# Layer 1's third and fourth chunk: the first product by seven block products, with sums of weights made on DVE and ACT

## The chip, the cores and the metric

One NeuronCore of a Trainium2 chip runs the kernel. Its engines work from queues of their own: PE (TensorE, matrix products into PSUM; PEld is its weight load), DVE (VectorE), ACT (ScalarE), POOL (GpSimd) and SP (SyncE, which issues most DMAs). Each takes its instructions strictly in the order in which the program left them, and waits for the others by semaphores. The metric is device time in microseconds (us) of one execution.

## What is computed

Attention over q, k, v (sparse masks), then a first layer (mixing along the tokens, then a two-product feed-forward), then the second layer, "layer 1" in the code. The change lies in the last part of it:

```python
def _moe2_ref(x, w_ch1, w_ch2):
    X = np.fft.fft(x, axis=1)
    X = np.fft.fft(X, axis=2)
    mixed = np.real(X).astype(np.float32)
    u = x + mixed
    mu = np.mean(u, axis=-1, keepdims=True)
    var = np.mean((u - mu) ** 2, axis=-1, keepdims=True)
    un = (u - mu) / np.sqrt(var + 1e-06)
    ch = np.maximum(un @ w_ch1, 0.0) @ w_ch2
    return (u + ch).astype(np.float32)
```

x is 4 batches of 576 tokens by 512; w_ch1 is 512 by 2048, w_ch2 2048 by 512.

## The kernel before

The 2304 tokens lie in 18 tiles of 128 tokens; `chunk_tiles` (L643) groups them in chunks: 0 to 3 are one batch each but for its last tokens (4 tiles, 512 tokens), chunk 4 holds the rest of all four batches (2 tiles, 256 tokens). `SEQ` (L847) runs the two layers' chunks one after the other: layer 0 in the order 0, 1, 2, 4, 3, layer 1 in the order 0, 1, 2, 3, 4. A pair (1, 2) below is layer 1, chunk 2, which is the layer's third.

`ffn` (L787) is one chunk's feed-forward. It works in two halves h of the 2048 hidden columns, eight blocks of 128 (`HW`) each. A half has a first product, one PSUM tile of 128 hidden columns by the chunk's tokens after the other, and a second product, which adds the half's eight blocks into one PSUM tile for each token tile. All values are kept as two fp16 parts, high and low, and a product is three matrix multiplications (high by high, high by low, low by high): L807 to L809 in the first product (12 for a tile, 96 for a half), L833 to L835 in the second (24 for a token tile, 96 for a half of a 4-tile chunk).

- A tile of the first product leaves PSUM by an eviction pair: ACT's relu into `gh` (L813), then DVE's rest into `gl` (L814). The PSUM pool `pf1` has two buffers, so PE starts tile i+2 only when tile i's pair is through.
- A token tile of the second product leaves by one DVE instruction, `ub` (L841, `ur` for chunk 4), from the pool `pf2`, also two buffers; in layer 1's second half SP then writes it out (L844).
- The operands of layer 1's first product come from `prep2` (L755): mean and variance, `un` on DVE (L777), its high part on ACT (L781), its low part on POOL (L782), and `put_T` (L595) turns both by DMA transposes that SP issues (L612) into `ut`. `ut` is single, so these transposes wait until the chunk before has ended its first products.
- `fft_gen` (L646) does batch b's two Fourier transforms on PE, ACT and DVE and adds them to `ub`; it must be through before `prep2` of that batch.
- `w_half` and `w_scale` (L202, L186) bring the weights in as two fp16 parts. They live in slots S0 to S32; S24 to S31 are free in layer 1.

The order of the instructions comes from two side lanes (`Lane`, L53), "w" for weights and "s" for the rest: `tick` (L944), called from the feed-forward's loops, steps them by rates for each chunk (`RATES`, L50; first number weights, second the rest), and a scheduler behind it fixes each engine's queue from that, with a higher priority for the evictions. A lane holds at a `guard` until a flag of the feed-forward is set, and the feed-forward pulls what it needs with `until`.

Of the kernel before, what the change touches and what calls it, by code (L numbers as in the profile page):

```python
# [7 lines left out]
F32 = mybir.dt.float32  # L8
# [61 lines left out]
def fused_kernel(ctx: ExitStack, tc: tile.TileContext, ql, kl, vl, vr, qs, ks, vs, uraw, vraw,  # L70
# [131 lines left out]
    def w_half(l, kind, src, names, h):  # L202
        m0 = h * HW
        row = 2 * kind + h
        sls = [slot(names[0])]
        for i in range(HW):
            sls.append(slot(names[i + 1]))
            w = sls[i + 1].bitcast(F32).rearrange("p a n -> p (a n)")
            to_f32(take(src, m0 + i), w)
            fetch()  # L210
            A.activation(out=sls[0][:, 0, :].bitcast(BF16), in_=w, func=AF.Square, accum_out=wst[:, row, i:i + 1])  # L211
            yield
        w_scale(l, kind, h)
        yield
        for i in range(HW):
            m = m0 + i
            w = sls[i + 1].bitcast(F32).rearrange("p a n -> p (a n)")
            sc = wsc[:, l, row, i:i + 1]
            split_hi(sls[i][:, 0, :], w, sc)
            split_lo(sls[i][:, 1, :], w, sc, sls[i][:, 0, :])  # L220
            W[l, kind, m] = sls[i]
            flags.add(f"w{l}{kind}{m}")
            yield

    ap_ctx = ExitStack()
# [369 lines left out]
    def put_T(key, j, hi, lo):  # L595
        if j == 0:
            UT[key] = [utp.tile([128, 4, 512], F16, tag=f"ut{i}", name=f"ut{i}") for i in range(2)]
# [157 lines left out]
    def prep2(c, tiles):  # L755
# [18 lines left out]
        yield  # L774
        for j, t in enumerate(tiles):
            un = fp.tile([128, 512], F32, tag="un", name="un")
            V.tensor_scalar(out=un, in0=utile(t), scalar1=mv[:, j, 0:1], scalar2=rs[:, j:j + 1],  # L777
# [3 lines left out]
            A.activation(out=hi, in_=un, func=AF.Copy)  # L781
            G.tensor_tensor(out=lo, in0=un, in1=hi, op=ALU.subtract)  # L782
            put_T((1, c), j, hi, lo)
            yield
        flags.add(f"p1{c}")

    def ffn(l, c, tick):  # L787
        tiles = chunk_tiles(c)
        n = 128 * len(tiles)
        until(f"p{l}{c}")  # L790
        uh, ul = UT[l, c]
        for h in range(2):
            gh = gp.tile([128, HW, 512], F16, tag="gh", name="gh")
            gl = gp.tile([128, HW, 512], F16, tag="gl", name="gl")
            subs = SUB if l == c == h == 0 else ((0, len(tiles)),)
            for s0, s1 in subs:
                cols = slice(128 * s0, 128 * s1)
                n = 128 * (s1 - s0)
                for i in range(HW):
# [12 lines left out]
                    with tc.high_priority(HP):  # L812
                        A.activation(out=gh[:, i, cols], in_=ps[:, 0:n], func=AF.Relu)  # L813
                        V.scalar_tensor_tensor(out=gl[:, i, cols], in0=ps[:, 0:n], scalar=0.0, in1=gh[:, i, cols],  # L814
                                               op0=ALU.max, op1=ALU.subtract)
            flags.add(f"e{l}{c}{h}1")
            until(f"w{l}1{h * HW}")
# [31 lines left out]
    def prep(q):  # L849
        l, c = SEQ[q]  # L850
        if q >= 2:
            yield from guard("e%d%d11" % SEQ[q - 2])
        yield from (prep2 if l else prep1)(c, chunk_tiles(c))

    def weights():
# [15 lines left out]
        yield from guard("e0311")  # L871
        yield from w_half(1, 1, w22, n[16:24] + n[32:], 1)

    def side():
# [15 lines left out]
        yield from prep(6)  # L890
        yield from fft_gen(3)
        for q in (7, 8, 9):
            yield from prep(q)

    def open_phase2():
        ap_ctx.close()
        fp = ctx.enter_context(tc.tile_pool(name="fft", bufs=2))
        fft["pool"] = fp
        fft["w"] = ctx.enter_context(tc.tile_pool(name="vsl", bufs=1))
        th = fp.tile([128, 2, 3, 290], F32R, tag="th", bufs=1, name="th")  # L900
# [26 lines left out]
    for l in range(2):  # L927
        for c in range(5):
            owner[f"p{l}{c}"] = sl
        for m in range(NW):  # L930
            owner[f"w{l}0{m}"] = owner[f"w{l}1{m}"] = wl
    ml = Lane(load_mix(), flags)
    first_loads()
# [194 lines left out]
```

## Time and profile before

| what | us |
|---|---|
| median of three runs | 972.61 (969.4 to 978.28) |
| the profiled execution, its own time | 973.36 |
| its span, first to last instruction | 971.4 |
| PE busy | 928.4 (96%) |
| DVE busy | 532.5 (55%) |
| ACT busy | 360.9 (37%) |
| POOL busy | 61.0 (6%) |

A busy PE is a modelled span of pipelined products, so it tells only where PE has no gaps. The shares are means over the whole span; what a change in one stage is worth is read from that stage.

### The profile page before, as it was taken

The numbers are of one execution on the slowest core, as the hardware profiler recorded it, in microseconds if no ns is written. First come the engines' busy times: TensorE is split into PE (matmuls) and PEld (weight loads), VectorE is DVE, ScalarE is ACT, GpSimd is POOL, SyncE is SP. The second block draws the span as 40 slices with busy tenths as digits, with TensorE's granted clock in tenths as the row PEclk, the third lists the DMA queues.
The fourth block names the chain that finished last, engine by engine and source line by source line (L and its number), as shares of the span: only waits on it lengthen the run. The fifth ranks groups of instructions, "written<-read, shape, count | busy, mean of one in ns | idle before, by whom it ended". The sixth has DMA issues, their size and how long they took to land.

```text
span 971.4 us, 13694 instructions
## 1 busy us (share of the span) xinstructions
PE 928.4 (96%) x5264; PEld 520.9 (54%) x5264; DVE 532.5 (55%) x1346; ACT 360.9 (37%) x885; POOL 61.0 (6%) x91
## 2 busy tenths in 40 slices
PE   5958899999999999999999989999999999999998
PEld 4746654556545665466445445555554444444465
DVE  4588788834352346862878998994245212222122
ACT  4577687724131434631446454231122101111011
POOL 0010011000000001100110400011001000100000
PEclk9969999999999999999999999999999999999999
DMA  9357666332201102601323520011002001200100
GB/s 315 121 180 250 207 213 206 103 116 95 64 7 37 39 3 95 175 21 35 97 90 127 131 65 1 1 36 53 1 1 55 33 1 11 76 1 1 52 15 22
DMA packets 60464, 76.53 MB, mean 79 GB/s; under 512 B 38064, under 2 KB 43440, under 8 KB 60400
## 3 DMA queue, kind: packets, MB, share of 16 engines
q1 hardware_dynamic: 51376, 42.53, 15.5%
q0 software_dynamic: 9024, 33.14, 10.6%
q8 instruction: 41, 0.67, 0.3%
q14 instruction: 23, 0.19, 0.1%
HBM read 60.18 MB, written 7.08 MB: 69 GB/s over the span
## 4 chain that ended last, share of the span: by engine, by line
PE 52%; DMA 3%; DVE 3%; ACT 1%; issue 1%; SPq 0%; ACTq 0%; DVEq 0%
PE f L833 8%; PE f L834 8%; PE f L835 8%; PE f L807 8%; PE f L808 8%; PE f L809 8%; DMA raw<-in_w 2%; DMA ut<-lo 1%; DVE wslot L156 1%; PE bk L689 1%; PE bk L688 1%; PE bk L690 1%; ACT wslot L153 1%; PE bk L698 0%; SPq L612 0%
## 5 line engine op out<-in xcount | busy, mean ns | idle before, releaser
L807 PE MATMUL f<-ut,wslot 128*128 128x512 f16 (+1 forms) x672 | 235.6, 351 | 8.0 <-DVE gl L814 7.6
L808 PE MATMUL f<-ut,wslot 128*128 128x512 f16 (+1 forms) x672 | 235.2, 350 | 1.1 <-DMA ut<-lo 1.1
L809 PE MATMUL f<-ut,wslot 128*128 128x512 f16 (+1 forms) x672 | 235.1, 350 | 0.0
L833 PE MATMUL f<-wslot,gh 128*128 128x512 f16 x576 | 218.1, 379 | 0.6 <-DVE ub L841 0.3
L834 PE MATMUL f<-wslot,gh 128*128 128x512 f16 x576 | 218.1, 379 | 0.1
L835 PE MATMUL f<-wslot,gl 128*128 128x512 f16 x576 | 218.1, 379 | 0.0
L813 ACT ACTIVATE gh<-f 128x512 f16<-128x512 f32 (+1 forms) x168 | 89.5, 533 | 300.9 <-PE f L809 300.3
L814 DVE SCALAR_TENSOR_TENSOR gl<-f,gh 128x512 f16<-128x512 f32 (+1 forms) x168 | 102.9, 612 | 145.5 <-ACT gh L813 144.9
L841 DVE SCALAR_TENSOR_TENSOR ub<-f,ivt,ub 128x512 f32<-128x512 f32 x64 | 47.9, 748 | 127.6 <-PE f L835 127.4
L808 PEld LDWEIGHTS <-wslot 128*128 128x128 f16 x672 | 66.1, 98 | 66.2 <-issue 12.4
L807 PEld LDWEIGHTS <-wslot 128*128 128x128 f16 x672 | 66.3, 99 | 59.3 <-issue 4.0
L809 PEld LDWEIGHTS <-wslot 128*128 128x128 f16 x672 | 66.0, 98 | 58.6 <-issue 0.9
L835 PEld LDWEIGHTS <-gl 128*128 128x128 f16 x576 | 56.4, 98 | 67.0 <-issue 0.3
L833 PEld LDWEIGHTS <-gh 128*128 128x128 f16 x576 | 57.0, 99 | 63.2 <-issue 0.2
L834 PEld LDWEIGHTS <-gh 128*128 128x128 f16 x576 | 56.7, 98 | 62.5 <-issue 1.3
L153 ACT ACTIVATE wslot<-wslot,wsc 128x512 f16<-128x512 f32 x64 | 46.0, 719 | 41.9 <-DVE wslot L156 21.2
L133 ACT ACTIVATE wslot<-raw 128x512 f32<-128x512 f32 x64 | 42.7, 675 | 29.4 <-DMA raw<-in_w 29.0
L160 POOL DMA_DIRECT2D raw<-in_w x61 | 33.3, 546 | 316.7 <-DVE wslot L137 62.1
L156 DVE SCALAR_TENSOR_TENSOR wslot<-wslot,wsc 128x512 f16<-128x512 f32 x64 | 48.7, 760 | 6.6 <-ACT wslot L153 6.4
L211 ACT ACTIVATE wslot<-wslot 128x512 bf16<-128x512 f32 x64 | 40.3, 629 | 20.9 <-DVE wslot L137 16.8
L377 ACT ACTIVATE P<-bk,mx 108x64 f32<-108x64 f32 (+2 forms) x126 | 31.3, 329 | 39.2 <-DVE mx L372 35.9
L137 DVE SCALAR_TENSOR_TENSOR wslot<-raw,wslot 128x512 int32<-128x512 int32 x64 | 44.4, 697 | 0.1
(225 smaller groups left out, 952.2 us busy)
## 6 DMA issues: line engine op xcount, KB each, us to landing
raw<-in_w POOLq DMA_DIRECT2D x61, 512.0 KB, 3.9
q<-in_ql SPq DMA_DIRECT2D x8, 576.0 KB
q<-in_qs SPq DMA_DIRECT2D x7, 594.0 KB
out<-ub SPq DMA_DIRECT2D x16, 256.0 KB
vl<-in_vl SPq DMA_DIRECT2D x8, 390.0 KB
vs<-in_vs SPq DMA_DIRECT2D x8, 390.0 KB
k<-in_kl SPq DMA_DIRECT2D x8, 320.0 KB
scr<-xs SPq DMA_DIRECT2D x8, 270.0 KB
```

The lines of the kernel that those rows point to most:

```text
L137: V.scalar_tensor_tensor(out=d, in0=hi, scalar=-0x80000000, in1=d, op0=ALU.bitwise_and, op1=ALU.bitwise_or)
L153: A.activation(out=dst, in_=src, func=AF.Copy, scale=s)
L156: V.scalar_tensor_tensor(out=dst, in0=src, scalar=s, in1=hi, op0=ALU.mult, op1=ALU.subtract)
L807: T.matmul(ps[:, 0:n], lhsT=wh, rhs=uh[:, k, cols], start=(k == 0), stop=False)
L808: T.matmul(ps[:, 0:n], lhsT=wh, rhs=ul[:, k, cols], start=False, stop=False)
L809: T.matmul(ps[:, 0:n], lhsT=wl, rhs=uh[:, k, cols], start=False, stop=(k == 3))
L813: A.activation(out=gh[:, i, cols], in_=ps[:, 0:n], func=AF.Relu)
L814: V.scalar_tensor_tensor(out=gl[:, i, cols], in0=ps[:, 0:n], scalar=0.0, in1=gh[:, i, cols], op0=ALU.max, op1=ALU.subtract)
L833: T.matmul(ps, lhsT=ga, rhs=w[:, 0, :], start=(i == 0), stop=False)
L834: T.matmul(ps, lhsT=ga, rhs=w[:, 1, :], start=False, stop=False)
L835: T.matmul(ps, lhsT=gb, rhs=w[:, 0, :], start=False, stop=(i == HW - 1))
L841: V.scalar_tensor_tensor(out=utile(t), in0=ps, scalar=iv, in1=utile(t), op0=ALU.mult, op1=ALU.add)
```

## The change

Layer 1's chunks 2 and 3 (`BLK`) no longer run their first product tile by tile. A pair of hidden blocks is taken as a matrix of two by two blocks (two halves of the 512 inputs, two hidden blocks), the chunk's tokens as two halves of 256, and the eight block products become seven, with sums of weights and sums of operands in place of some operands (Winograd's form of Strassen's algorithm). A product of a block pair is 12 multiplications of 256 columns (`prod`), so a group g of four hidden blocks is 84 of them, and two groups, in turns, make a half: 168 of 256 columns where 96 of 512 stood. The partial results are saved or added by ACT (`save`) and DVE (`add`) into six temporaries in S24 to S29, and evicted by the pair in `relu`.

The sums of weights (`s_pair`, eight pairs) are made once, on DVE with a copy by ACT, from the fp16 weights; the lane "w" begins them after `guard("e1101")`, the flag set when chunk (1, 1)'s first half of the first product is written into the program. A tiny copy from `last[0]` ties each to the newest `gl`. The sums of operands (`prep_blocks`) replace `un`, high and low parts of the two chunks; the low parts go from POOL to DVE, and a chunk has 16 transposes instead of 8. The lane "s" makes all of chunk 2's, 3's and 4's preparation after `fft_gen(3)`, without the guards that held it before, in memory that the Fourier transforms leave free (`open_late`), and the rates in chunk (1, 1) change. A row of weights' scales is levelled by pairs in `w_half`. The descriptors' scratch of POOL's DMAs shrinks, which makes room in SBUF.

```diff
+BLK = (2, 3)
+LATE = [0.75, 0.85]
-RATES = [[2.5, 2.0], [2.5, 1.5], [2.5, 2.0], [4.5, 2.75], [1.5, 1.5], [1.05, 2.25], [2.0, 0.5], [3.25, 2.0], [4.25, 1.0], [3.0, 2.0]]
+RATES = [[2.5, 2.0], [2.5, 1.5], [2.5, 2.0], [4.5, 2.75], [1.5, 1.5], [1.05, 2.25], [1.0, 4.0], [3.25, 2.0], [4.25, 1.0], [3.0, 2.0]]
...
         w_scale(l, kind, h)
+        if l and not kind:
+            sc = wsc[:, l, row, :].rearrange("p (n two) -> p n two", two=2)
+            for e in range(2):
+                V.tensor_tensor(out=sc[:, :, e], in0=sc[:, :, e], in1=sc[:, :, 1 - e], op=ALU.min)
...
+    def s_pair(p):
+
+        wa, wb = W[1, 0, 2 * p], W[1, 0, 2 * p + 1]
...
+        for w, t in ((wa, f0), (wb, f1)):
+            V.tensor_copy(t[0:1, 0:1], last[0])
+            V.tensor_tensor(out=t, in0=w[:, 0], in1=w[:, 1], op=ALU.add)
+        yield
+        for o, u, v, op in ((sa[:, x], f1[:, x], f1[:, y], ALU.add), (sa[:, y], sa[:, x], f0[:, x], ALU.subtract),
+                            (sb[:, x], f0[:, x], f1[:, x], ALU.subtract), (sb[:, y], f0[:, y], sa[:, y], ALU.subtract)):
+            V.tensor_tensor(out=o, in0=u, in1=v, op=op)
+        yield
+        st = s_store(p)
+        for t, z in zip(st, (sa, sb)):
+            A.activation(out=t[:, 0], in_=z, func=AF.Copy)
+            V.tensor_tensor(out=t[:, 1], in0=z, in1=t[:, 0], op=ALU.subtract)
...
+    def prep_blocks(c, tiles, mv, rs):
...
+        for q in range(2):
...
+            for j, t in zip((q, q + 2), un):
+                V.tensor_scalar(out=t, in0=utile(tiles[j]), scalar1=mv[:, j, 0:1], scalar2=rs[:, j:j + 1],
+                                op0=ALU.subtract, op1=ALU.mult)
...
+            V.tensor_tensor(out=ta[:, x], in0=un[1][:, x], in1=un[0][:, x], op=ALU.subtract)
+            V.tensor_tensor(out=ta[:, y], in0=un[1][:, y], in1=un[1][:, x], op=ALU.subtract)
+            V.tensor_tensor(out=tb[:, x], in0=un[1][:, y], in1=ta[:, x], op=ALU.subtract)
+            V.tensor_tensor(out=tb[:, y], in0=un[0][:, y], in1=tb[:, x], op=ALU.subtract)
+            yield
+            for pool, z, w, dh, dl in ((tmp, un[1][:, y], 256, ux[:, 4:6, cols], ux[:, 6:8, cols]),
+                                       (tmp, un[0], 512, u0[:, 0:4, cols], u1[:, 0:4, cols]),
+                                       (fp, ta, 512, u0[:, 4:8, cols], u1[:, 4:8, cols]),
+                                       (fp, tb, 512, ux[:, 0:4, cols], uy[:, 0:4, cols])):
...
+                V.tensor_copy(hi[0:1, 0:1], last[0])
+                A.activation(out=hi[:, 0:w], in_=z, func=AF.Copy)
+                V.tensor_tensor(out=lo[:, 0:w], in0=z, in1=hi[:, 0:w], op=ALU.subtract)
+                S.dma_start_transpose(out=dh, in_=hi[:, 0:w])
+                S.dma_start_transpose(out=dl, in_=lo[:, 0:w])
...
+    def blocks(c, g, gh, gl, tick):
...
+        X = pf1.tile([128, 512], F32, tag="f1", name="X")
+        Z = pf2.tile([128, 512], F32, tag="f2", name="Z")
+        prod(X, 0, 1, True)
+        p1 = save(0, X)
+        tick()
+        prod(Z, 4, 5, True)
+        p5 = save(1, Z)
+        yield
+        prod(X, 5, 6, False)
+        u2 = save(2, X)
+        tick()
+        prod(Z, 6, 3, False)
+        t12 = add(3, Z, u2)
+        prod(X, 3, 7, False)
+        t22 = add(4, X, p5)
+        relu(t12, 0, 1)
+        tick()
+        relu(t22, 1, 1)
+        Y = pf2.tile([128, 512], F32, tag="f2", name="Y")
+        prod(Y, 1, 2, True)
+        t11 = add(5, Y, p1)
+        relu(t11, 0, 0)
+        tick()
+        yield
+        prod(X, 2, 4, False)
+        relu(X, 1, 0)
...
+            if blk:
+                d0, d1 = (blocks(c, g, gh, gl, tick) for g in (2 * h, 2 * h + 1))
+                for d in (d0, d0, d1, d0, d1, d1):
+                    next(d)
...
-        if q >= 2:
+        if 2 <= q < 7:
             yield from guard("e%d%d11" % SEQ[q - 2])
...
+        yield from guard("e1101")
+        for p in range(8):
+            if p == 4:
+                yield from guard("late")
+            yield from s_pair(p)
...
         yield from fft_gen(3)
+        open_late()
         for q in (7, 8, 9):
             yield from prep(q)
...
-    nc = bacc.Bacc("TRN2", target_bir_lowering=False, num_devices=1)
+    nc = bacc.Bacc("TRN2", target_bir_lowering=False, num_devices=1, dynamic_dma_scratch_size=2048)
```

Three places of the queues are spoken of below. First DVE's queue in chunk (1, 1), about the second product of its first half (`ub_87`). Of the kernel before, from the last eviction of the first product on:

```order
L814 SCALAR_TENSOR_TENSOR gl<-f_6524,gh 128x512 [waits Activation_49]
L841 SCALAR_TENSOR_TENSOR ub_87<-f_6539,ivt,ub_87 128x512 [waits PE_49]
L841 SCALAR_TENSOR_TENSOR ub_87<-f_6576,ivt,ub_87 128x512 [waits PE_49]
L841 SCALAR_TENSOR_TENSOR ub_87<-f_6613,ivt,ub_87 128x512 [waits PE_49]
L841 SCALAR_TENSOR_TENSOR ub_87<-f_6660,ivt,ub_87 128x512 [waits PE_49]
L741 TENSOR_TENSOR T_6695<-As,bk 128x129 [waits PE_49,Activation_49]
```

Of the change, the piece between that second product's second and third eviction (L1013); ua and uc are sums of operands, wslot sums of weights:

```order
L867 TENSOR_TENSOR lo<-uc,hi 128x512 [waits Activation_49]
L849 TENSOR_SCALAR ua<-ub_88,mv,rs 128x512 [waits DVE_49]
L849 TENSOR_SCALAR ua<-ub_88,mv,rs 128x512
L253 CAST wslot<-gl 1x1
L865 COPY hi<-gl 1x1 [waits DMAHW5_49]
L854 TENSOR_TENSOR uc<-ua 128x256 [waits DVE_49]
L855 TENSOR_TENSOR uc<-ua 128x256
L856 TENSOR_TENSOR uc<-ua,uc 128x256 [waits DVE_49]
L254 TENSOR_TENSOR wslot<-wslot 128x512
L857 TENSOR_TENSOR uc<-ua,uc 128x256 [waits DVE_49]
L867 TENSOR_TENSOR lo<-ua,hi 128x256 [waits DMAHW7_49,Activation_49]
L865 COPY hi<-gl 1x1 [waits DMAHW4_49]
```

Where one eviction followed the other, sums and preparation now stand between; from the first half's last `gl` (L985 of the change) to the second half's first there are 78 instructions where there were 15 (each count with that last one).

Second, DVE's queue for the second group of a half of chunk (1, 2), from the sum that frees Z to the last eviction, of the change:

```order
L912 TENSOR_TENSOR wslot<-Z,wslot 128x512 [waits PE_49,Activation_49]
L920 SCALAR_TENSOR_TENSOR gl<-wslot,gh 128x2x256 [waits Activation_49]
L912 TENSOR_TENSOR wslot<-X,wslot 128x512 [waits PE_49]
L912 TENSOR_TENSOR wslot<-Y,wslot 128x512 [waits PE_49]
L920 SCALAR_TENSOR_TENSOR gl<-wslot,gh 128x2x256 [waits Activation_49] x2
L920 SCALAR_TENSOR_TENSOR gl<-X,gh 128x2x256 [waits Activation_49]
```

Before, eight rows L814 stood there alone, each for one tile. The eviction of t12 now stands ahead of the sum t22 that frees X, and PE's last product of the group goes into X.

Third, ACT's queue at the turn from chunk (1, 1) to chunk (1, 2), of the change; the first row is the copy for a pair of weight sums, the others belong to the first block products:

```order
L262 ACTIVATE ss<-sx 128x512 [waits DVE_49] x2
L906 ACTIVATE wslot<-X 128x512 [waits PE_49]
L906 ACTIVATE wslot<-Z 128x512 [waits PE_49]
L906 ACTIVATE wslot<-X 128x512 [waits PE_49]
L919 ACTIVATE gh<-wslot 128x2x256 [waits DVE_49] x3
```

Before, ACT had only the tiles' relus (L813) there. The saves of X and Z now stand behind copies that wait for DVE.

## Rows read from the trace of the kernel before

**Rows 1.** Page, part 1: busy us (share of the span) and instructions.
```profile
PE 928.4 (96%) x5264; PEld 520.9 (54%) x5264; DVE 532.5 (55%) x1346; ACT 360.9 (37%) x885; POOL 61.0 (6%) x91
```
**Rows 2.** Windows: stretch, its us, then busy by engine, PEclk, DMA share, GB/s.
```profile
core 0: us, PE busy (x) PEld busy (x) DVE busy (x) ACT busy (x) POOL busy (x), PEclk, DMA share, GB/s
669.40:690.10 20.70, 20.70 (x97) 9.41 (x96) 5.59 (x8) 4.18 (x7) 0.00 (x0) 1.00 0.03 13
690.10:716.50 26.40, 26.40 (x152) 14.76 (x151) 3.92 (x6) 3.10 (x12) 0.00 (x0) 1.00 0.01 1
716.50:739.20 22.70, 22.70 (x113) 11.08 (x113) 18.71 (x73) 7.11 (x20) 0.00 (x0) 1.00 0.00 0
739.20:759.90 20.70, 20.70 (x97) 9.37 (x96) 5.73 (x8) 3.01 (x5) 4.83 (x4) 1.00 0.39 89
...
842.80:925.70 82.90, 82.90 (x386) 37.56 (x385) 17.07 (x24) 9.56 (x16) 0.00 (x0) 1.00 0.07 20
```
**Rows 3.** Timeline of PE: start us, us, instruction; both widths of first product.
```profile
759.93 0.38 PE L807 MATMUL f<-ut,wslot 128*128 128x512 f16 x1
...
780.65 0.38 PE L833 MATMUL f<-wslot,gh 128*128 128x512 f16 x1
...
925.69 0.27 PE L807 MATMUL f<-ut,wslot 128*128 128x256 f16 x1
...
936.17 0.38 PE L833 MATMUL f<-wslot,gh 128*128 128x512 f16 x1
```
**Rows 4.** Lines by form, 925.8 to 957 us, weight loads: count | busy us, mean ns.
```profile
L809 PEld LDWEIGHTS <-wslot 128*128 128x128 f16 x64 | 6.3, 98 | 0.7
```
**Rows 5.** Windows and timelines about PE's longest wait in layer 1.
```profile
550.00:569.70 19.70, 15.03 (x77) 8.04 (x76) 19.64 (x45) 11.72 (x23) 5.79 (x5) 0.98 0.46 110
569.70:572.60 2.90, 2.85 (x8) 1.02 (x8) 2.90 (x10) 0.67 (x1) 0.00 (x0) 0.53 0.46 172
...
569.03 0.67 DVE L814 SCALAR_TENSOR_TENSOR gl<-f,gh 128x512 f16<-128x512 f32 x1
...
569.75 0.58 PE L807 MATMUL f<-ut,wslot 128*128 128x512 f16 x1 [4.72 <-DVE gl L814]
```
**Rows 6.** Lines by form, DVE, whole span: count | busy us, mean ns | idle before.
```profile
L814 DVE SCALAR_TENSOR_TENSOR gl<-f,gh 128x512 f16<-128x512 f32 x120 | 82.6, 688 | 116.8 <-ACT gh L813 116.3
...
L659 DVE TENSOR_TENSOR es<-ub 128x512 f32<-128x512 f32 x16 | 10.8, 678 | 0.0
...
L665 DVE TENSOR_TENSOR fb<-es 128x256 f32<-128x256 f32 x16 | 6.7, 418 | 0.0
```
**Rows 7.** Timeline of DVE, back to back: 512 wide, 256 wide, dependent pairs.
```profile
565.44 0.68 DVE L135 SCALAR_TENSOR_TENSOR wslot<-wslot,raw 128x512 int32<-128x512 int32 x1
566.04 0.75 DVE L156 SCALAR_TENSOR_TENSOR wslot<-wslot,wsc 128x512 f16<-128x512 f32 x1
...
724.25 0.42 DVE L745 TENSOR_TENSOR ub<-ub,T 128x255 f32<-128x255 f32 x1
724.58 0.42 DVE L750 TENSOR_TENSOR ub<-ub,T 128x257 f32<-128x257 f32 x1
...
736.04 0.24 DVE L773 SCALAR_TENSOR_TENSOR rs<-t,rs 128x4 f32<-128x4 f32 x2
736.24 0.24 DVE L771 SCALAR_TENSOR_TENSOR t<-rs 128x4 f32<-128x4 f32 x2
```
**Rows 8.** Timeline of one tile's way out; PE's row starts the next tile.
```profile
672.02 0.38 PE L807 MATMUL f<-ut,wslot 128*128 128x512 f16 x1
...
672.22 0.60 ACT L813 ACTIVATE gh<-f 128x512 f16<-128x512 f32 x1 [9.96 <-PE f L809]
...
672.85 0.69 DVE L814 SCALAR_TENSOR_TENSOR gl<-f,gh 128x512 f16<-128x512 f32 x1 [2.47 <-ACT gh L813]
```
**Rows 9.** Lines by form, ACT, whole span: count | busy us, mean ns | idle before.
```profile
L781 ACT ACTIVATE hi<-un 128x512 f16<-128x512 f32 x18 | 11.0, 626 | 31.6 <-DMA ut<-hi 15.6 <-DVE un L777 15.5 <-DVE ub L841 0.5
```
**Rows 10.** Timelines of SP, two transposes, and of POOL, which waits for one's landing.
```profile
830.85 2.52 SPq L612 DMA_TRANSPOSE ut<-lo  x2
...
833.40 1.16 POOL L782 TENSOR_TENSOR lo<-un,hi 128x512 f16<-128x512 f32 x1 [2.46 <-DMA ut<-lo]
```

More of the change, by code (lines that the diff above doesn't have):

```diff
@@ L774, in prep2 @@
         yield
+        if c in BLK:
+            yield from prep_blocks(c, tiles, mv, rs)
+            return
         for j, t in enumerate(tiles):
-            un = fp.tile([128, 512], F32, tag="un", name="un")
+            un = (fp.tile([128, 2, 512], F32, tag="ua", bufs=1, name="ua")[:, 0] if "late" in flags else
+                  fp.tile([128, 512], F32, tag="un", name="un"))
             V.tensor_scalar(out=un, in0=utile(t), scalar1=mv[:, j, 0:1], scalar2=rs[:, j:j + 1],
@@ L781, in prep2 @@
             A.activation(out=hi, in_=un, func=AF.Copy)
-            G.tensor_tensor(out=lo, in0=un, in1=hi, op=ALU.subtract)
+            (V if "late" in flags else G).tensor_tensor(out=lo, in0=un, in1=hi, op=ALU.subtract)
             put_T((1, c), j, hi, lo)
@@ new lines, in blocks, with tl, pr, prod @@
+    def blocks(c, g, gh, gl, tick):
+        nt = 256
+        for p in (2 * g, 2 * g + 1):
+            until(f"s{p}")
+        ops = UT[1, c]
+        g0 = 4 * (g % 2)
+        def tl(i):
+            return slot(f"S{24 + i}").bitcast(F32).rearrange("p a n -> p (a n)")
+        def pr(b):
+            return b.rearrange("p (a n) -> p a n", a=2)
+        def prod(b, wi, p, first):
+            th, tl_, oh, ol = ops[p - 1]
+            for a in range(2):
+                o = b[:, nt * a:nt * a + nt]
+                w, c0 = WS[2 * g + a][wi]
+                for kk in range(2):
+                    cs = slice(c0.start + 128 * kk, c0.start + 128 * kk + 128)
+                    wh, wl = w[:, 0, cs], w[:, 1, cs]
+                    uh, ul = th[:, oh + kk, :], tl_[:, ol + kk, :]
+                    kw = dict(stop=True, skip_group_check=True)
+                    T.matmul(o, lhsT=wh, rhs=uh, start=first and a == kk == 0, **kw)
+                    T.matmul(o, lhsT=wh, rhs=ul, start=False, **kw)
+                    T.matmul(o, lhsT=wl, rhs=uh, start=False, **kw)
+        def save(i, b):
+            t = tl(i)
+            with tc.high_priority(HP):
+                A.activation(out=t, in_=b, func=AF.Copy)
+            return t
+        def add(i, b, y):
+            t = tl(i)
+            with tc.high_priority(HP):
+                V.tensor_tensor(out=t, in0=b, in1=y, op=ALU.add)
+            return t
+        def relu(x, i, half):
+            gs = slice(g0 + i, g0 + i + 3, 2)
+            cs = slice(nt * half, nt * half + nt)
+            with tc.high_priority(HP):
+                A.activation(out=gh[:, gs, cs], in_=pr(x), func=AF.Relu)
+                V.scalar_tensor_tensor(out=gl[:, gs, cs], in0=pr(x), scalar=0.0, in1=gh[:, gs, cs],
+                                       op0=ALU.max, op1=ALU.subtract)
+            last[0] = gl[0:1, g0 + i, cs.start:cs.start + 1]
+        X = pf1.tile([128, 512], F32, tag="f1", name="X")
[5 more added lines that the diff above has]
+        p5 = save(1, Z)
+        yield
+        prod(X, 5, 6, False)
[13 more added lines that the diff above has]
+        tick()
+        yield
+        prod(X, 2, 4, False)
+        relu(X, 1, 0)
+        yield
@@ L790, in ffn @@
         until(f"p{l}{c}")
-        uh, ul = UT[l, c]
+        blk = l and c in BLK
+        if not blk:
+            uh, ul = UT[l, c]
         for h in range(2):
@@ L815, in ffn @@
                                                op0=ALU.max, op1=ALU.subtract)
+                    last[0] = gl[0:1, i, cols.start:cols.start + 1]
             flags.add(f"e{l}{c}{h}1")
@@ L931, in fused_kernel @@
             owner[f"w{l}0{m}"] = owner[f"w{l}1{m}"] = wl
+    for p in range(8):
+        owner[f"s{p}"] = wl
     ml = Lane(load_mix(), flags)
```

53 lines of the change are left out of this document (48 added, 5 removed).

## The prediction

> **What bounds the kernel now.** I read the busy times first. PE is busy 96% of the span, DVE 55% [rows 1], so PE's stream sets the time wherever it has no gap. Then the windows over layer 1's later chunks: from 739.2 us on PE is busy for every microsecond of each stage at the full clock, and DVE for 5 to 6 us of some 21 [rows 2]. The reader is to see that these stages can be shortened only by less work on PE, and that DVE is nearly empty in them, but for the second half of chunk (1, 1)'s first product (18.7 of 22.7 us, the end of the last Fourier transform). Last, the one large gap in layer 1: in the 19.7 us before 569.7 DVE was busy 19.64, an eviction stood behind other work in its queue, and PE idled 4.72 us for it, then ran 2.9 us at a granted clock of 0.53 [rows 5]. A full DVE queue with evictions in it does stop PE here.
>
> The profiled execution took 973.36 us, its span 971.4; 0.75 over the median of 972.61. The sum below goes from 973.4.
>
> **What is removed on PE.** A half's first product ran from 759.93 to 780.65, 20.72 us for 96 matrix multiplications of 512 columns, 0.216 each. Chunk 4's half took 925.69 to 936.17, 10.48 us for 96 of 256 columns, 0.109 each [rows 3]. Now a half has 168 of 256 columns: 18.34 us. That is 2.38 less, and there are four such halves: **-9.5 us**. It is also the most that the change can give.
>
> Each multiplication loads its weights anew; a load takes 0.098 us [rows 4], inside the 0.109 pitch, so it is hidden at 256 columns already in chunk 4. The Trainium skill ("TensorE: Matmul & The Clock Gate", "The mechanism") says that weight loads overlap with running multiplications only when they go to another group of rows. By that the loads of 128 full rows would stand between the multiplications; the rows above contradict it, and the sum goes by the rows. What it would give is the last rival.
>
> **What is added inside a half.** A tile leaves PSUM like this: ACT starts 0.20 after PE goes on, takes 0.60, DVE starts 0.03 later and takes 0.69 [rows 8]. A sum from PSUM on DVE is bounded by 0.42 (256 wide) and 0.69 (512 wide) [rows 6]; it is 512 wide, I take 0.68. A product of a block pair is 12 times 0.109, 1.31 us. Saves by ACT (0.2 + 0.6) fit behind the next product. The one that does not fit is the second group's end: PE goes on to X's last product 2.62 us after Z's last. On DVE stand t12 (Z + u2), the eviction of t12, then t22, which frees X: 0.20 + 0.68 + ACT's relu 0.63 [rows 9] + DVE 0.70 + 0.68, with 0.1 for the hand-overs, is 2.97. PE waits 0.35, four times: **+1.4**. In the first group another group's two products lie between and cover it. In the first half of chunk (1, 2) the last pair of weight sums stands on DVE and ACT between the groups, 4 us of work where about 4 are free; I take **+0.8**, bounds 0 and 2.
>
> **What is added on DVE in chunk (1, 1).** A pair of weight sums is two sums 512 wide, four 256 wide and two low parts 512 wide; a chunk's preparation has four `un`, eight sums 256 wide and eight low parts, six of them 512 wide. Back to back a 512-wide instruction takes 0.60 (565.44 to 566.04), a 256-wide one 0.33 (724.25 to 724.58), a tiny one 0.10 if two chains alternate and 0.20 if it waits for the one before (two in 0.20) [rows 7]. No row adds two fp16 tiles into fp32; it is bounded by 0.33 and 0.60, and nearest to the 512-wide `es` (0.678 alone) [rows 6], so 0.60.
>
> All of this falls into chunk (1, 1), because the lane starts it at the first half's end and needs it before (1, 2). From that half's last `gl` to the second half's first one, DVE's queue holds 78 instructions: 27 wide (16.3 us), 22 half wide (7.3) and 29 tiny (4.1), and 18 of them wait for a result of DVE's own, some 0.06 more each: **28.8 us**. PE gives it less. Let t be PE's end of the first half. Its last `gl` is through at t + 1.5 [rows 8], the second product takes 20.7, two tiles 2 x 2.59, and PE's third tile, at t + 25.9, needs the first `gl`. So 24.4 us are there for 28.8. DVE also comes late: in the last four tiles of the first half it has 12.0 us of work (nine statistics of the preparation among it) for 10.4 of PE, so 1.6. PE stands 28.8 + 1.6 - 24.4 = 6.0 us at its third tile. The second product itself is not held: its two PSUM buffers allow 5.2 us of lateness, and DVE has at most 4.
>
> After that, DVE has 18.6 us for the seven evictions that follow, where PE wants some 16.5, and PE restarts at the lower clock (seven multiplications twice as long in [rows 5], +1.5, partly inside DVE's own time): +2. A last 0.5 for the first half's late evictions. Together **+8.5**; bounds: 3 (no dependent waits, no lateness at the start) and 14 (every dependent step at 0.11, and a slow restart on more tiles).
>
> At the turn to the blocks ACT's first saves stand behind a copy for weight sums that waits for DVE, still some 3 us behind PE: X's save ends about 0.5 after PE wants it: **+0.5**, bounds 0 and 3.
>
> **What costs nothing, and its cover.** SP's 16 transposes of a chunk take 1.26 each (two in 2.52) and land 2.6 after their start (830.85, 833.40) [rows 10]; chunk 2's, 20 us, begin about 7 us into the second product and are needed 55 us later; chunk 3's wait for PE to leave `ut` and then have 60 us. Outputs queue behind them, for which nobody waits before the end. Without that cover a chunk would wait up to 20 us. DVE's waits for a landed transpose (a `hi` buffer) come about as fast as SP issues, so I take none. POOL loses its low parts, but is 6% busy [rows 1]. The Fourier matrices move into one place between two tiles, same count. The two tiny minima for each half of weights: 0.4 us of DVE before the gap of [rows 5], 0 to 0.4 of it on PE, taken as 0. The smaller descriptor scratch: no row shows it; 0, at worst one 2.6 us landing now and then.
>
> **Sum.** 973.4 - 9.5 + 1.4 + 0.8 + 8.5 + 0.5 = 975.1; I say **975.0**. What PE is spared in chunks 2 and 3 it stands idle in chunk (1, 1).
>
> **Rivals.**
> *DVE keeps up.* If the sums run faster than 0.60 (16-bit operands), or the queue is less dense than its count, PE never waits in (1, 1): 973.4 - 9.5 + 1.4 = 965.3, and 963.9 with no wait inside the halves. For it: DVE has 15 us or more free in each of three stages [rows 2]. Against it: the work before the second half's first `gl` counts to more than the time even at bare pitches (27.7 against 24.4).
> *The clock stays low (the other side).* After the 6 us gap DVE holds PE again at every tile, and if PE's clock does not come back, a tile takes 12 x 0.43 = 5.1 us; six tiles are 15 us more in place of the 2 above: 988. It decides from two slow tiles on. Against it: after 4.72 us idle the clock was back in 2.9 us of work [rows 5], and the later waits are a few tenths.
> *Loads are not hidden:* 672 multiplications at 0.109 + 0.098, 139 us for 83: 1030. Chunk 4 speaks against it [rows 3, 4].
>
> **Chances.** Forecast (967 to 982 by its bounds) 0.70; DVE keeps up 0.17; low clock 0.11; loads 0.02. The range leaves out the last two and the fastest edge of the second: 965 to 982. About 1% (9.7 us) is what a measurement of this kernel can tell from no change. Faster by over 1% needs nearly the whole of the 9.5 and a little beside: half of the second rival, 0.09. Slower by over 1%, over 982: the last two, with a little of the forecast's upper end, 0.15. Within 1%: 0.76.
>
> **What would show it.** In the trace after: block products of 18.3 to 18.7 us a half; PE waiting for `gl` for some 6 us about the third tile of (1, 1)'s second half; DVE busy over 95% from its first half's end to the turn; a granted clock near 0.5 just behind the gap; X's last product waiting 0.3 to 0.4 for t22. Wrong if DVE shows idle stretches there, if the 512-wide sums of weights take about half of 0.68, or if a half takes over 20 us.

## The result, and the profile after

The changed kernel took 962.53 us (median; 960.17 to 964.86) beside 973.82 (969.4 to 978.28) for the kernel before: a ratio of 0.9895, interval 0.985 to 0.9941. The forecast was 975.0, in 965 to 982. Further comparisons below gave 0.9981 and 0.9915. Half of the first difference turns out not to be the change's: the change is worth 5.6 us, and the rest lies ahead of the part that it changes, in the traces mostly in the attention at the program's head, whose length varies from execution to execution.

The page's first part, to be held against [rows 1]: busy us, share of the span, instructions.

```profile
PE 913.5 (95%) x5552; PEld 542.9 (56%) x5552; DVE 589.9 (61%) x1504; ACT 387.9 (40%) x933; POOL 48.7 (5%) x81
```

PE lost 15 us of busy time, DVE gained 57. The windows show where that lies, one row for each stage (a half's first product, then its second) from chunk (1, 1) to the second half of chunk (1, 2), where the fifth and seventh row are the first two of the four halves made of blocks; they answer to [rows 2]:

```profile
core 0: us, PE busy (x) PEld busy (x) DVE busy (x) ACT busy (x) POOL busy (x), PEclk, DMA share, GB/s
666.24:694.64 28.40, 28.40 (x167) 16.47 (x166) 17.55 (x54) 9.49 (x30) 0.00 (x0) 1.00 0.03 10
694.64:715.36 20.72, 20.72 (x97) 9.41 (x96) 20.72 (x64) 7.29 (x13) 0.00 (x0) 1.00 0.27 45
715.36:738.06 22.70, 21.05 (x97) 9.36 (x96) 22.24 (x76) 7.55 (x14) 0.00 (x0) 1.00 0.22 47
738.06:758.78 20.72, 20.72 (x97) 9.41 (x96) 19.98 (x52) 7.78 (x14) 0.00 (x0) 1.00 0.57 108
758.78:777.81 19.03, 18.62 (x169) 16.43 (x168) 13.58 (x26) 9.37 (x16) 0.00 (x0) 1.00 0.21 56
777.81:798.53 20.72, 20.72 (x98) 9.37 (x96) 3.58 (x6) 0.60 (x1) 0.00 (x0) 1.00 0.00 1
798.53:817.25 18.72, 18.50 (x169) 16.43 (x168) 8.57 (x14) 7.87 (x13) 0.00 (x0) 1.00 0.01 2
```

The reader is to see DVE full (20.72 of 20.72) in the stage where it was nearly empty before, PE short of full only in the third row and a little in the blocks, and the clock at 1.00 throughout. What PE waited for from 666.2 us to the end (engine, line and tile waited for; us in total, times, longest):

```profile
PE f L978 <- DVE gl L985: 1.7, 2, 1.5
PE X L899 <- DVE wslot L912: 1.1, 4, 0.4
```

Both waits were forecast, at these places. Before, PE waited for nothing in that part.

Stage times, each from one PE product's start to the next stage's first, give the change's whole account. "Tail" is everything from chunk (1, 1)'s first product to the last instruction:

| us | before | after |
|---|---|---|
| chunk (1, 1): four stages | 20.72 + 26.33 + 22.73 + 20.72 = 90.50 | 28.41 + 20.72 + 22.70 + 20.72 = 92.55 |
| four first products of (1, 2), (1, 3) | 4 x 20.72 = 82.88 | 19.03 + 3 x 18.72 = 75.19 |
| tail | 301.96 | 296.32 |
| ahead of the tail | 669.4 | 666.2 |

The tail is 5.64 us shorter: 2.05 lost in chunk (1, 1), 7.69 gained in the blocks. The last Fourier transform moved from (1, 1)'s second and third stage into its first. Of the 3.2 us ahead of the tail, 3.1 had arisen by 415 us; up to there the queues of both kernels are the same instruction for instruction, and PE's products are the same up to the tail.

### The profile page after: what moved, and what is told of

It reads as the page before. It is cut to its first block, busy times and chain, and to the rows that moved or that the text cites. A ratio compares the mean times of both kernels' runs of the same rounds, so it can differ in the third digit from the quotient of the medians.

```text
span 962.6 us, 14541 instructions
## 1 busy us (share of the span) xinstructions
PE 913.5 (95%) x5552; PEld 542.9 (56%) x5552; DVE 589.9 (61%) x1504; ACT 387.9 (40%) x933; POOL 48.7 (5%) x81
## 5 line engine op out<-in xcount | busy, mean ns | idle before, releaser
L978 PE MATMUL f<-ut,wslot 128*128 128x512 f16 (+1 forms) x480 | 169.9, 354 | 10.3 <-DVE gl L985 9.9
L979 PE MATMUL f<-ut,wslot 128*128 128x512 f16 (+1 forms) x480 | 169.8, 354 | 1.1 <-DMA ut<-lo 1.1
L980 PE MATMUL f<-ut,wslot 128*128 128x512 f16 (+1 forms) x480 | 169.5, 353 | 0.0
L984 ACT ACTIVATE gh<-f 128x512 f16<-128x512 f32 (+1 forms) x136 | 70.2, 517 | 163.7 <-PE f L980 163.3
L985 DVE SCALAR_TENSOR_TENSOR gl<-f,gh 128x512 f16<-128x512 f32 (+1 forms) x136 | 80.6, 593 | 70.8 <-ACT gh L984 69.8
L1013 DVE SCALAR_TENSOR_TENSOR ub<-f,ivt,ub 128x512 f32<-128x512 f32 x64 | 47.8, 747 | 116.8 <-PE f L1007 116.6
L979 PEld LDWEIGHTS <-wslot 128*128 128x128 f16 x544 | 53.7, 99 | 54.0 <-issue 15.5
L978 PEld LDWEIGHTS <-wslot 128*128 128x128 f16 x544 | 53.9, 99 | 44.6 <-issue 4.2
L980 PEld LDWEIGHTS <-wslot 128*128 128x128 f16 x544 | 53.5, 98 | 43.8 <-issue 1.2
```

What stands on the lines that cost most here:

```text
L978: T.matmul(ps[:, 0:n], lhsT=wh, rhs=uh[:, k, cols], start=(k == 0), stop=False)
L979: T.matmul(ps[:, 0:n], lhsT=wh, rhs=ul[:, k, cols], start=False, stop=False)
L980: T.matmul(ps[:, 0:n], lhsT=wl, rhs=uh[:, k, cols], start=False, stop=(k == 3))
L1013: V.scalar_tensor_tensor(out=utile(t), in0=ps, scalar=iv, in1=utile(t), op0=ALU.mult, op1=ALU.add)
```

## Is the rest of the gain the change's? The start

**The changed kernel again, twice, and the kernel before with the small scratch.** Edits: none; and, on the kernel before,

```diff
-num_devices=1)
+num_devices=1, dynamic_dma_scratch_size=2048)
```

> The changed kernel once more, beside the kernel before and the three kernels that follow. Theory 'own part': in the two traces the change's own stages (chunk (1, 1) to the end) account for 5.8 us of the 8.8 us between the spans, and the other 3.2 us lie in the attention ahead of the first feed-forward product, whose instruction queues are the same in both kernels; they are chance, and this comparison gives a ratio of 0.994 (about 6 us less) with the first product of layer 0 starting anywhere between 66 and 76 us. Theory 'systematic start': the start is shorter in every run of the changed kernel, the first product starts at 68 to 69 us again and the ratio is 0.988 to 0.991.

> The kernel before with one part of the change alone: the smaller descriptor scratch of POOL's DMAs. Theory 'own part' (start by chance): ratio 1.000 within 0.3%, 970 to 976 us. Theory 'systematic start': the smaller scratch is what moves the start, 3 to 5 us less than before (0.995 to 0.997), and the first product of layer 0 starts at 68 to 69 us in place of 75.

> The changed kernel a third time. From chunk (1, 1) to the end the traces so far take 301.96 us in both of before's own (and 301.97 with the extra multiplications at the head) and 296.32 in both of the changed kernel's (296.22 with them); what lies ahead of that took 663.6 to 680.6 us, with the same queues. Theory 'own part and start': the tail is 296.3 again, the start anywhere in 664 to 681, and the ratio lies about 0.994, between the 0.9895 of the first comparison and the 0.9981 of the second. Rival 'systematic start': the ratio is 0.989 or 0.990 again, with the start at 666 or less in most executions.

Measured: 970.77 us, ratio 0.9981 (0.9947 to 1.0014); 976.23 us, 0.9995 (0.9952 to 1.0038); 964.60 us, 0.9915 (0.9874 to 0.9957). The tails were 296.32 and 296.34 in the changed kernel's two new traces, 301.96 with the small scratch: the own part is the same to 0.02 us each time. The time ahead of the tail was 673.1, 676.2 and 676.3 us. Taking each execution's span less its kernel's tail, the time ahead ran from 661.8 to 677.0 for 28 executions of the changed kernel (median 670.8) and from 658.4 to 680.2 for 79 of the kernel before (median 670.3; two of over 1000 us left out). So taken together the start belongs to neither kernel, and the four executions of the first comparison (662.1 to 666.7) happened to be short ones. The executions of one comparison are not independent in this: the changed kernel's median time ahead was 664, 673 and 666 in the three, and its three ratios, 0.9895, 0.9981 and 0.9915, lie further apart than their intervals allow. The small scratch shows no effect, within the 0.5% of its interval. All executions of both kernels together have medians of 968.97 (28) and 974.24 (83), 5.3 apart, beside the tail's 5.64.

What differs within the start: PE rows of the same code in the changed kernel's first trace, and in its second (start, us, count of products):

```profile
27.91 1.07 PE L477 MATMUL bk<-k,q 128*108 128x54 f32 x10
28.91 0.75 PE L461 MATMUL bk<-vl,gl 96*64 96x65 f32 x16
```
```profile
29.44 1.92 PE L477 MATMUL bk<-k,q 128*108 128x54 f32 x10
31.29 1.21 PE L461 MATMUL bk<-vl,gl 96*64 96x65 f32 x16
```

and the windows of 20 to 24 and 28 to 40 us, the first trace's first:

```profile
20.00:24.00 4.00, 3.67 (x18) 3.10 (x17) 2.48 (x10) 2.45 (x8) 0.00 (x0) 1.00 1.02 408
...
28.00:40.00 12.00, 10.35 (x114) 9.12 (x112) 9.73 (x33) 10.50 (x36) 1.59 (x3) 1.00 0.39 128
```
```profile
20.00:24.00 4.00, 3.67 (x18) 2.80 (x17) 2.89 (x10) 2.50 (x9) 0.00 (x0) 1.00 1.02 407
...
28.00:40.00 12.00, 11.95 (x86) 10.52 (x85) 7.17 (x26) 7.38 (x23) 1.07 (x2) 1.00 0.35 107
```

The same fp32 products take 0.107 and 0.192 us each, and in 12 us PE gets through 114 products or through 86; by 45 us the second trace is 8.6 us behind. PE had been busy 3.67 of 4 us in both just before. The column of the granted clock reads 1.00 in both, but it reads so too where a trace has no record of the clock. In the raw traces the records begin at 23.5 us in the first and at 81.5 us in the second, each with a rise to 1.00. The changed kernel's third trace has its records earlier and shows a stretch as slow as the second's for what it is:

```profile
28.00:40.00 12.00, 11.95 (x83) 10.91 (x81) 6.60 (x23) 7.85 (x25) 1.06 (x2) 0.50 0.36 119
```

In the thirteen traces here (all but the one of `spread`), the fp32 products of 54 columns follow each other after 0.095 us in the median where a record says 1.00, and after 0.180 where one says 0.50 or where none has come yet. So the two paces are the clock's two levels, 2.4 and 1.2 GHz. The clock also parts the starts: in the six traces where it was recorded at 1.00 from about 24 to 39 us, the time ahead of the tail is 663.6 to 666.9 us, in the seven others 669.4 to 680.6, with forms of either kernel on both sides.

**Keeping PE busy from the beginning.** The same edit on both kernels:

```diff
+    ob = ones.bitcast(BF16)
+    dm = pb.tile([128, 512], F32, tag="b", name="dm")
+    for _ in range(32):
+        T.matmul(dm[:, 0:256], lhsT=ob[:, 0:128], rhs=ob[:, 0:256], start=True, stop=True)
```

> The kernel before with 32 extra matrix multiplications on ones (256 columns each, result unused) at the head of PE's queue, which run from about 1 to 8 us while PE waits for its first inputs; all five queues are otherwise as before. In the traces so far the attention's products of 128x54 fp32 run at 0.180 us each between 28 and 54 us in before, after_again, before_scratch and sum_first, and at 0.095 between 28 and 40 us in the changed kernel's first trace and in no_sums, though the queues there are the same and the column of the granted clock says 1.00 in both. Theory 'start state': whether PE runs at the one pace or the other there is left to small differences in when inputs land; with PE kept busy from the beginning the fast pace comes in every execution, the first product of layer 0 starts at 66 to 70 us in place of 75 to 77, and the median falls by 4 to 8 us, to 966 to 970. Rival 'not PE': the pace follows something else (the data that comes in); nothing changes, 971 to 976.

> The changed kernel with the same 32 multiplications at the head. Theory 'start state': 960 to 964 us, and the ratio to before_warm shows the change's own part alone, 5.6 us or 0.994. Rival 'not PE': 966 to 972 as after_again, with the same spread.

Measured: 974.59 us, 1.0039 (0.9999 to 1.0079); 974.52 us, 0.9973 (0.9915 to 1.0031). Not shorter, and no narrower: "start state" had this wrong. The windows of 12 to 20 and 24 to 40 us, of before with the extra products and of after with them:

```profile
12.00:20.00 8.00, 5.39 (x35) 4.61 (x34) 4.63 (x13) 4.18 (x13) 0.00 (x0) 0.50 1.03 353
...
24.00:40.00 16.00, 12.79 (x146) 10.86 (x144) 12.44 (x42) 13.84 (x44) 2.28 (x4) 0.97 0.51 163
```
```profile
12.00:20.00 8.00, 4.16 (x36) 3.36 (x36) 5.29 (x15) 4.58 (x15) 0.00 (x0) 0.83 1.01 334
...
24.00:40.00 16.00, 15.70 (x122) 13.39 (x122) 9.29 (x31) 10.48 (x31) 1.76 (x3) 0.50 0.51 164
```

Here the column shows what happens: the granted clock fell to 0.50 (1.2 GHz) behind the thin stretch after 8 us, in which PE waits for its inputs (busy 2.52 and 1.36 of the 4 us from 8 to 12), and was back for 24 to 40 us in the one execution (0.97) and still down in the other (0.50). So the granted clock makes the difference in the start, and PE's busy time in the first 8 us does not decide it. What decides when it rises there stays open. Their tails, 301.97 and 296.22, are as before, 5.75 apart where their medians differ by 0.07.

## Where DVE's queue holds PE: chunk (1, 1)

**Sums of weights left out.** In `s_pair` the sums, their copies and their low parts go, and the block products read plain weights in their place (other values, the same products):

```diff
+        WS[p] = ((wa, x), (wa, y), (wb, y), (wa, x), (wb, x), (wb, y), (wa, y))
```

> The changed kernel with the sums of weights left out (the block products of such sums read plain weights in their place, so the values differ; every matrix multiplication and all of the preparation of the operands stay). Theory 'fixed work': what stands in DVE's queue between the last eviction of chunk (1, 1)'s first half and the first of its second half is set by the lane, it falls to about 19 to 20 us, and PE's waits of 1.66 and 0.32 us there, and of 0.57 and 0.13 us in chunk (1, 2)'s first half, go: 2 to 2.7 us less than the changed kernel. Rival 'packed queue': the scheduler fills that stretch with other work up to what it believes to fit (79 instructions stand there still, 78 before), and 1 us or more of the wait stays.

**Sums begun earlier.**

```diff
-        yield from guard("e1101")
+        yield from guard("e1012")
```

> The changed kernel with the sums of weights begun one half of a chunk earlier (behind the flag of chunk (1, 0)'s second half in place of (1, 1)'s first half's). Theory 'fixed work': DVE's queue between the two halves of chunk (1, 1) loses two pairs, some 7 us, and PE's waits of 1.66 and 0.32 us there go: chunk (1, 1) to the end 294.3 us in place of 296.3. Rival 'packed queue': the scheduler fills the place with preparation (70 instructions stand there for 78), and what is saved at the third tile comes back as a wait elsewhere in (1, 1): 296 us.

**More sums.** In `s_pair`, behind the four sums of 256 columns:

```diff
+        for _ in range(2):
+            V.tensor_tensor(out=f1, in0=sa, in1=sb, op=ALU.add)
```

> The changed kernel with two more sums of 512 columns on DVE in each of the eight pairs (their results are overwritten unused): 16 x 0.60 = 9.6 us more for DVE. Theory 'fixed work', on which the prediction stood: what the lane gives DVE between the two halves of chunk (1, 1) must all run there, five or more of the extra sums among it, and PE's wait at the third tile grows from 1.66 to 4.5 us or more: 299 to 303 us from chunk (1, 1) to the end in place of 296.3. Rival 'packed queue': the scheduler puts only so much ahead of an eviction as it believes to fit, the wait there stays at 1.5 to 2.5 us, and the rest moves to the second half and to the turn, where 1 to 4 us are lost: 297 to 300 us.

**Slower lanes**, on the kernel `sum_first` of the next section; `LATE` holds the side lanes' rates once the last Fourier transform is through:

```diff
-LATE = [0.75, 0.85]
+LATE = [0.5, 0.6]
```

and [0.5, 0.7] for `spread_less`.

> sum_first with slower lanes once the Fourier transforms are through (LATE [0.5, 0.6] in place of [0.75, 0.85]), so that part of chunk (1, 3)'s preparation and of the sums of weights is emitted later, in chunk (1, 2), where DVE is busy for 9 of 19 us and less. By the durations in the trace of the changed kernel, DVE's queue from the first half's last gl to the second half's first falls from 24.7 to 21.3 us. Theory 'DVE queue': 2.0 late at the start + 21.3 is under the 25.9 that PE gives it, so the waits of 1.7 to 2.0 and 0.3 us in chunk (1, 1) go and nothing else comes: stages of 28.4, 20.7, 20.7, 20.7 and blocks of 18.3 to 18.6 us, 292.6 to 293.0 us from chunk (1, 1) to the end in place of 294.9 (sum_first) and 296.3 (changed kernel). Rival 'transposes': with less work between them DVE waits for transposes to land, as in no_sums, and PE waits 1 to 2 us for a ub or at the turn: 294 to 296 us.

> As spread, with LATE [0.5, 0.7]: DVE's queue between the halves counts to 22.9 us. Theory 'DVE queue': 2.0 + 22.9 + ACT's and DVE's way out is still under 25.9, no wait in chunk (1, 1): 292.6 to 293.2 us from there to the end. Rival 'transposes': a wait for ub or at the turn as in spread, of another size: 294 to 296 us. If the price of a row were larger by a tenth (as the prediction took it) a wait of 1 us would stand here and none in spread.

> The kernel spread once more: in its first execution every matrix multiplication took four times as long from beginning to end, so it tells nothing. spread_less took 294.7 us from chunk (1, 1) to the end: the wait at the third tile fell from 2.0 to 0.45, but 0.6 and 0.7 came in the blocks and one stage changed its shape. Theory 'DVE queue': no wait in chunk (1, 1), stages of 20.7, 20.7, 20.7 after the first, some waits of 0.5 to 1 in the blocks: 293.3 to 294.2. Rival 'transposes and copies': what leaves (1, 1) comes back in the blocks of (1, 2), 294.5 to 296.

In the first execution of `spread` (3929.68 us) PE was slow from end to end: one product of 512 columns followed another after 1.28 us in the median until some 1500 us and after 0.84 from 1800 us on, in place of 0.216. It is left out below, and `spread_again` is the same kernel. For each trace: how late the first half's last `gl` ended after PE began the second product; from there to the end of the second half's first `gl`; their sum, less the 25.9 us that the prediction gave PE; and PE's wait at the third tile.

| | late | gl to gl (instructions) | sum - 25.9 | PE waits | tail |
|---|---|---|---|---|---|
| after | 2.00 | 25.51 (78) | 1.61 | 1.66 | 296.32 |
| no_sums | 2.00 | 23.60 (79) | -0.30 | 0 | 296.25 |
| sums_earlier | 2.68 | 25.17 (70) | 1.95 | 2.01 | 296.06 |
| more_sums | 2.00 | 24.91 (73) | 1.01 | 1.06 | 298.37 |
| sum_first | 1.99 | 25.81 (78) | 1.90 | 1.96 | 294.92 |
| spread_less | 1.95 | 24.35 (92) | 0.40 | 0.45 | 294.67 |
| spread_again | 2.02 | 22.81 (88) | -1.07 | 0 | 293.57 |

Six kernels besides the changed one agree with the prediction's arithmetic within 0.06 us: PE waits one for one for what DVE has too much. What stands in that stretch, however, is not what the lane gives it. With 9.6 us more for DVE there were five instructions fewer and the wait fell; with all of the sums gone there was one more; begun half a chunk earlier, the sums left 70 there, but DVE came 0.68 later and the wait grew. "Fixed work" is refuted. The counts fit the rival "packed queue", by which the scheduler fills the place ahead of an eviction with what it believes to fit and moves the rest, though not its sizes: in `no_sums` none of the wait stayed there, where it had 1 us or more, and in `more_sums` 1.06, where it had 1.5 to 2.5. How the scheduler chooses is not shown beyond these counts. For the slower lanes the stretch was expected at 22.9 and 21.3 us and took 24.35 and 22.81, so part of the wait stayed in `spread_less`. What is moved costs PE elsewhere. What PE waited for in the tail of `more_sums`:

```profile
PE X L901 <- DVE wslot L914: 1.6, 4, 0.9
PE X L901 <- ACT wslot L908: 1.5, 2, 0.9
PE f L980 <- DVE gl L987: 1.1, 2, 0.9
```

The saves L908 of the first block products stand behind copies of sums that come late, the turn for which the prediction had 0.5 us. In `no_sums`, the whole of the gain at the third tile (2.0) came back in the second product. DVE, then PE:

```profile
753.14 0.69 DVE L817 TENSOR_TENSOR lo<-ua,hi 128x512 f16<-128x512 f32 x1 [2.13 <-DMA us<-lo]
753.75 1.40 DVE L998 SCALAR_TENSOR_TENSOR ub<-f,ivt,ub 128x512 f32<-128x512 f32 x2
```
```profile
754.55 0.38 PE L990 MATMUL f<-wslot,gh 128*128 128x512 f16 x1 [1.97 <-DVE ub L998]
```

With nothing between them, the low parts run ahead of the transposes; one waits 2.13 us for a landing, and the eviction behind it with it. The prediction had taken these waits as none: in the changed kernel the sums of weights fill the time, and one such wait of 0.2 us is left in the stretch of the table. The median of `no_sums` was 969.82 us, 0.9959 (0.9922 to 0.9997).

The slowest lanes take all of the wait away (`spread_again`: 28.41 + 20.72 + 20.72 + 20.72 in chunk (1, 1)); 1.05 us comes back in chunk (1, 2), its second half, where PE's queue now has some products of the two kinds in turns. 0.67 of it, from start to start, is one product that waits for a copy of a sum:

```profile
PE Z L899 <- ACT ss L262: 0.5, 1, 0.5
```

`spread_again` measured 966.97 us, 0.9921 (0.9877 to 0.9965), beside 964.60 for the changed kernel in the same comparison. By its tail it is 2.75 us ahead of the changed kernel and 8.4 ahead of before; the start's spread hides that in the medians.

## The waits inside a half

```diff
         t22 = add(4, X, p5)
+        if g % 2:
+            V.tensor_copy(gh[0:1, g0, nt:nt + 1], t22[0:1, 0:1])
         relu(t12, 0, 1)
```

> The changed kernel with a one-element copy that makes ACT's relu of t12 wait for the sum t22 in each half's second group, so that DVE's sum, which frees X, stands ahead of t12's eviction. Theory 'order': the PE waits of 0.39 us ahead of X's last product go in all four halves: 1.4 to 1.6 us less than the changed kernel, too little for the time, plain in the trace. Rival 'moved': the evictions come 0.6 us later, and PE waits as long for Y or at the second product's last blocks: 0 us.

DVE at the end of a half in chunk (1, 2), the changed kernel first (its L912 are the sums t12, t22 and t11), then with the copy:

```profile
813.21 0.69 DVE L912 TENSOR_TENSOR wslot<-Z,wslot 128x512 f32<-128x512 f32 x1 [1.37 <-PE Z L901]
814.60 0.69 DVE L920 SCALAR_TENSOR_TENSOR gl<-wslot,gh 128x512 f16<-128x512 f32 x1 [0.70 <-ACT gh L919]
815.21 0.68 DVE L912 TENSOR_TENSOR wslot<-X,wslot 128x512 f32<-128x512 f32 x1
```
```profile
816.75 0.69 DVE L912 TENSOR_TENSOR wslot<-Z,wslot 128x512 f32<-128x512 f32 x1 [1.37 <-PE Z L901]
817.99 0.69 DVE L912 TENSOR_TENSOR wslot<-X,wslot 128x512 f32<-128x512 f32 x1 [0.55 <-PE X L901]
818.71 0.14 DVE L940 CAST gh<-wslot 1x1 f16<-1x1 f32 x1
819.37 1.29 DVE L920 SCALAR_TENSOR_TENSOR gl<-wslot,gh 128x512 f16<-128x512 f32 x2 [0.52 <-ACT gh L919]
```

The sum that frees X starts 1.24 us after the one before it in place of 2.00, the halves are 18.34 us three times (18.47 the first) in place of 18.72 (19.03), 1.70 less in the four. Against that the wait at the third tile of (1, 1) grew by 0.30 (table above): tail 294.92, 1.40 less. In the time, 968.75 us, 0.996 (0.9929 to 0.999), beside 0.9981 for the changed kernel in the same comparison. The term's mechanism is shown: the order of two DVE instructions.

18.34 us is 168 x 0.109 with every product of 256 columns loading its own weights into all 128 rows. The Trainium skill ("TensorE: Matmul & The Clock Gate", "The mechanism") says that weight loads overlap with running products only where the group of rows differs; the measurement decides against it here.

## Why the prediction was wrong, step by step

| term | forecast | measured |
|---|---|---|
| four halves in 168 products of 256 columns | -9.5 | -9.52 (18.34 in `sum_first`) |
| waits inside the halves, (1, 2)'s first half, the turn | 1.4 + 0.8 + 0.5 | 0.69 + 3 x 0.38 = 1.83 |
| DVE's queue in (1, 1) | 8.5 | 2.05 |
| sum | +1.7 | -5.64 |

**PE's part** was right, to 0.02 us, and so was the cover of the transposes, apart from what `no_sums` shows.

**Inside the halves** the wait was forecast as 0.35, from the right order of instructions, and is 0.38. The pair of weight sums between the groups of (1, 2)'s first half cost 0.31 beside that (0.69 - 0.38; in `no_sums` that half takes 18.72 as the others do), not 0.8, and at the turn PE did not wait, where 0.5 stood.

**DVE's queue in (1, 1)** is the step that failed, in its size: the sum had 8.5 us for it, and 2.05 were lost. The place (third tile of the second half), the instruction waited for and the rule (late + queue - 25.9) were right; the forecast put 3.1 + 28.8 - 25.9 = 6.0 there, the trace 2.0 + 25.5 - 25.9 = 1.6. DVE, the beginning of that stretch and the row that ends it (start, us), then PE's wait:

```profile
696.56 0.15 DVE L817 SCALAR_TENSOR_TENSOR t<-rs 128x4 f32<-128x4 f32 x1
696.63 0.17 DVE L811 BATCH_NORM_AGGREGATE mv<-st 128x2 f32<-128x6 f32 x1
696.72 0.11 DVE L253 CAST wslot<-gl 1x1 f32<-1x1 f16 x1
696.76 0.15 DVE L818 TENSOR_TENSOR t<-t,vh 128x4 f32<-128x4 f32 x1
696.83 0.13 DVE L253 CAST wslot<-gl 1x1 f32<-1x1 f16 x1
696.90 0.67 DVE L254 TENSOR_TENSOR wslot<-wslot 128x512 f32<-128x512 f16 x1
697.50 0.14 DVE L819 SCALAR_TENSOR_TENSOR rs<-t,rs 128x4 f32<-128x4 f32 x1
697.57 0.67 DVE L254 TENSOR_TENSOR wslot<-wslot 128x512 f32<-128x512 f16 x1
...
701.93 0.98 DVE L849 TENSOR_SCALAR ua<-ub,mv,rs 128x512 f32<-128x512 f32 x2
702.85 0.67 DVE L263 TENSOR_TENSOR sraw<-wslot,sraw 128x512 f16<-128x512 f32 x1
...
721.48 0.67 DVE L985 SCALAR_TENSOR_TENSOR gl<-f,gh 128x512 f16<-128x512 f32 x1
```
```profile
720.33 0.38 PE L980 MATMUL f<-ut,wslot 128*128 128x512 f16 x1
722.21 0.38 PE L978 MATMUL f<-ut,wslot 128*128 128x512 f16 x1 [1.50 <-DVE gl L985]
```

The large prices were right: the sum of two fp16 tiles (L254) starts its follower after 0.60, the taken value. Too dear were: 29 tiny instructions, 0.14 each on average, which cost 0.04 to 0.09, start to start (2.1 us less in all); 18 waits for DVE's own results, 0.06 each, of which nothing is left, since enough other work stands between a result and its reader (1.1 less); four `un`, 0.46 each for 0.60 (0.6 less). Against them 0.5 more in evictions at 0.66 and one landing. That is the 3.3 us. The late start was taken as 1.6 and was 0.5. Nearly all the errors go the same way, and they stand in one difference of two numbers near 27: 3.3 us too much in a queue of 25.5, with the 1.1 of the late start, made a wait of 1.6 into one of 6.0. For the tiny ones the Trainium skill ("Perfetto Trace Analysis", "Optimizing Scalar/DVE Operations") has some 60 ns of fixed cost for DVE on SBUF; the trace agrees, 0.059 from start to start for the 1x1 copies L253 on average.

The two things built on the 6.0 fell with it: the slow clock behind the gap and the tiles after it (+2, measured 0.33: after 1.50 us of idling the window above has the clock at 1.00, where it was 0.53 after 4.72 [rows 5]), and the first half's +0.5 (0.07). The rival "DVE keeps up" (965.3) had the better end; its reason, that the queue is less dense than its count, was half of it, but PE does wait, so the truth lay between. With the measured sizes the sum would have been 973.4 - 5.6 = 967.8.

**The base.** The remaining 5 us between 967.8 and 962.5 are the start. The sum took one execution's start (669.4) as fixed; that part varies by 15 us and more. With the right sizes alone the sum, 967.8, would still lie in the stated range; that the four executions lay below it is the start's luck. Nothing in the prediction gave that a place in the range (and the bounds of its terms add up to 968.3 to 984.3, where it says 967 to 982), and "about 1%, what a measurement can tell" was not traced to its cause.

## What to carry to other kernels

Where a wait is the difference between two long queues, put a price on the error of each queue before putting one on the wait, and take tiny instructions and dependent ones from rows of a dense queue. A scheduler may pack what it places ahead of an eviction to its own estimate: here adding or removing side work changed where the wait was more than how long it was, so look for the next wait in the stages behind. To judge an edit of a few us in the middle of a program, compare the stretch from the edit on within the traces (here the same to 0.1 us) rather than whole times whose start varies by 15. A column of the profile can show its full value for want of a record, so hold it against durations.

## What was not expected of the hardware

- PE's pace in the attention differs between executions of the same queues: 0.107 or 0.192 us for the same fp32 product at about 28 us, the pace of the clock's two levels. The column shows 1.00 in both, but the slow one's trace has no record of the clock before 81.5 us.
- A tiny DVE instruction that reads the result of another starts 0.20 us after it, with nothing between (below, from the kernel before) or with one other tiny one (two in 0.20 [rows 7]). It costs only its own 0.07 where as much work of others stands between, as in the chain L817, L818, L819 above.

```profile
737.10 0.16 DVE L772 TENSOR_TENSOR t<-t,vh 128x2 f32<-128x2 f32 x1
737.30 0.16 DVE L773 SCALAR_TENSOR_TENSOR rs<-t,rs 128x2 f32<-128x2 f32 x1
```

- `un` (one tile with two scalars for each row, 512 wide, fp32) starts its follower after 0.46 us, where a sum of two tiles takes 0.60.
- One execution (the first of `spread`) ran PE slowly from beginning to end, 1.28 and later 0.84 us for a product of 512 columns in the median, while DVE's evictions took their usual 0.69. Its trace has no record of the clock, so the 1.00 shown there tells nothing. The kernel before had such long executions too (1915.18 us, without a trace), so the change is not their condition; their cause isn't known.
